# Expert weights loaded by halves, the recurrence's powers in a PSUM bank, and narrower expert slots

## The chip, the cores and the metric

One core of a Trainium2 chip. The metric is the device time of one execution in microseconds (us): the median of the runs shown. The engines are PE (TensorE), DVE (VectorE), ACT (ScalarE), POOL (GpSimd) and SP (SyncE, which here only issues DMAs). DMAs are issued from the queues of SP, ACT and POOL.

## The reference

A linear recurrence with a decay (RWKV) gives 3072 rows of 384 numbers; each row is then sent to one of 16 experts, chosen first by group and then within the group. All is fp32.

```python
# r, k, v: (4, 8, 768, 48); w, u: (8, 48)
for t in range(S):
    kt, vt, rt = (k[:, :, t], v[:, :, t], r[:, :, t])
    cur = np.einsum('bhd,bhe->bhde', u[None] * kt, vt)
    y[:, :, t] = np.einsum('bhd,bhde->bhe', rt, state + cur)
    state = w[None, :, :, None] * state + np.einsum('bhd,bhe->bhde', kt, vt)
# x = y as (3072, 384); w1: (4, 4, 384, 1024); w2: (4, 4, 1024, 384)
g_idx = argmax(x @ w_group);  e_idx = argmax(x @ w_expert[g_idx])
out[token] = softmax_weight_of_g * softmax_weight_of_e * (relu(x @ w1[g, e]) @ w2[g, e])
```

## The kernel before

**Tiles and steps.** The recurrence runs in 24 tiles of 128 tokens (`NT`), tile n being chunk c = n // 4 of batch b = n % 4; two tiles are a pair g. The loop over `s` (L852) is software-pipelined: step s turns tile s (`turn`, L710: PE transposes r into `pr` and the scaled k into `pk`; DVE makes `rT` = pr x T1T, ACT copies `kT`), makes the scores of tile s - 1 (`scores`, L723: PE, then DVE masks them into `am` by COPY_PREDICATED, L735), the values of tile s - 2 (`values`, L737: `py`, the state update `pu`) and turns back tile s - 3 (`back`, L783, with the routing logits). `am` is first filled by ACT with the diagonal (`own_scores`, L699): eight multiplications of the identity by `du`, the token's own product r u k. That comes from POOL (`own`, L686: `dg` = r x k, then x `ub`, which is u in all partitions) and a sum on DVE (`own_sum`, L694). POOL also scales k by the table T2 into `kh` (`scale_k`, L682).

**Tables.** `up_to` (L263) holds the powers of the decay w up to 128, made by four DVE scans. `backwards` (L285) makes the reversed powers `rev`, `turned` (L292) transposes them on PE into `ptab` and ACT copies that into T2; `powers` (L278) makes T1T. There is one table for each of three chunks (m = 0, 1, 2). At the start m = 0 is made on DVE, m = 1 on ACT; PE is kept busy by `warm` (products of ones) meanwhile.

**Loads.** r, k and v come in pairs into rings of four or five (`load_pair`, L144), from SP, with the first two k's from ACT. `rall` and `kall`, the rings of r and k, are later the place of the second expert's weights.

**Routing.** For groups of four tiles (the last four in twos) `route` (L377) chooses the expert of each row, its gate and its place, and POOL scatters rows of 386 numbers into regions of `x_sorted` (L457, one scatter a tile). After 16 tiles `pick_first` (L352) takes the two fullest experts, so that their weights can be loaded before the routing ends: at step 21 SP reads the number and sends for all of w1 of the first (four DMAs of 384 KB, L484), then, after the scatters of that time have landed, for part 0 of its rows (`load_rows`, L531) and all of w2 (1.5 MB, L489); at step 24 for w1 of the second. `columns(0)` (L556) turns the rows on DVE at step 24; `up(0, ...)` (L585) uses the first expert's w1 from step 25 on; `w2_part` (L477) copies w2 into the order of use, two of eight blocks at a time, three of the copies on POOL at step 25.

**Experts.** `ITEMS` (L509) are the expert slots: the fullest expert as two items, then one an expert, in falling order of counts. `SLOTS` are their widths in columns, fixed when the kernel is built; where a count is above its slot, a general path at the end does the rest (L1039). Each item is `up` (48 matmuls, three for each of 8 blocks and two passes, L596) and `down` (48 matmuls, L617), each as wide as the slot, so the time of PE goes with the width. The results go to `out` by scatters of POOL: in pieces (L656) and for the last item by rows (L669). In item i, SP sends for the rows of item i + 2 and, when `up` is through, for its w1 and w2 (L1033).

**Order.** Inside `manual_schedule` each engine runs its instructions in the order of the program; this covers all five engines up to L993, and PE and DVE in the experts. So whatever waits holds up all that stands behind it on its engine.

Of the kernel before, what the change touches and what calls it, by code (L numbers as in the profile page):

```python
# [15 lines left out]
P = 128  # L16
# [3 lines left out]
SLOTS = [256, 240, 233, 222, 216, 212, 206, 202, 199, 196, 193, 190, 187, 184, 178, 173]  # L20
# [14 lines left out]
def kernel(  # L35
# [88 lines left out]

    w2h = cst([HP, 2, DP], "w2h")
# [18 lines left out]
    def load_pair(g, k_queue=nc.sync):  # L144

        load(r, g, rts[g % RING][:, :, :, 0:D])
        load(k, g, kts[g % RING], k_queue)
        load(v, g, vts[g % (RING + 1)][:, :, :, 0:D])
# [18 lines left out]
    def turn_small():  # L167

        first, second = (
            gw_rows[:, BL * c : BL * (c + 1), :].rearrange("p d e -> p e d") for c in range(DP // BL)  # L170
        )
        nc.vector.transpose(gw_turned, first)
        for a in range(2):
            at = P // 2 * a
            nc.vector.transpose(gw_turned[at + BL : at + 2 * BL], second[at : at + BL])
        nc.scalar.copy(gw, gw_turned.rearrange("p e (m j) -> p j (e m)", j=HP))

    ub = cst([P, H, D], "ub")
    load_pair(0, nc.scalar)
    load_small()  # L180
    nc.scalar.dma_start(
        out=ub.rearrange("p h d -> p (h d)"), in_=bass.AP(tensor=u.tensor, offset=u.offset, ap=[[0, P], [1, H * D]])
    )
    load_pair(1, nc.scalar)
# [72 lines left out]
    nc.tensor.transpose(pw, w2h.rearrange("p e d -> p (e d)"), ident[0:HP, 0:HP])  # L257
    wc = cst([P, HP], "wc")
# [4 lines left out]
    up_to = cst([P, HP, P], "up_to")  # L263
# [14 lines left out]
    def powers(m, engine):  # L278
        for hc in range(HP):
            scaled(T1T[m][:, hc, :], up_to[:, hc, :], m, hc, engine)  # L280
# [4 lines left out]
    def backwards(m, engine):  # L285
        revs[m] = pool.tile([P, HP, P], FP32, name=f"rev_{m}")
        for hc in range(HP):
            x = up_to[:, hc, :]
            back = bass.AP(tensor=x.tensor, offset=x.offset + P - 1, ap=[list(x.ap[0]), [-1, P]])
            scaled(revs[m][:, hc, :], back, SPAN - 1 - m, hc, engine)  # L290

    def turned(m):  # L292
        ptab = bank([P, HP, P], "ptab")
        for hc in range(HP):
            nc.tensor.transpose(ptab[:, hc, :], revs[m][:, hc, :], ident)
        nc.scalar.copy(
            T2[m].rearrange("p (a e) d -> p a e d", e=2), ptab.rearrange("p a (e d) -> p a e d", e=2)[:, :, :, 0:D]
        )

    warm(5)  # L300
    backwards(0, nc.vector)
    turned(0)
    backwards(1, nc.scalar)
    nc.vector.reciprocal(by[:, 0, :], up_to[:, :, P - 1])
    nc.vector.tensor_mul(by[:, 0, :], by[:, 0, :], by[:, 1, :])
    powers(0, nc.vector)
# [13 lines left out]
    def span_decay():  # L320
        nc.gpsimd.tensor_mul(w_span, up_to[:, :, P - 1], up_to[:, :, P - 1])
        nc.gpsimd.tensor_mul(w_span, w_span, up_to[:, :, P - 1])
# [159 lines left out]
    def load_w1(e, i):  # L482
        for q in range(P // BL):
            nc.sync.dma_start(  # L484
                out=places[i][0][BL * q : BL * (q + 1)], in_=w1f[bass.ds(e, 1), q].rearrange("a p k f -> (a p) k f")
            )

    def load_w2(e, i):
        nc.sync.dma_start(out=places[i][1], in_=w2f[bass.ds(e, 1)].rearrange("a p k f -> (a p) k f"))  # L489

    def load_expert(e, i):

        load_w1(e, i)
        load_w2(e, i)
        return places[i]
# [32 lines left out]
    def padded(n):  # L528
        return -(-n // BL) * BL

# [32 lines left out]
    def keys_in(i):  # L563
# [4 lines left out]
        if is_last(i):  # L568
            for j, n in enumerate(parts(i)):
# [54 lines left out]
    def turn_out(i, d0, d1):  # L624

        if d0 == 0:
            out_rows[i] = [
                (bank([P, DM], "pb"), item_tile(i, [P, DM], "yt", bufs=4)) for j in range(len(parts(i)))
            ]
        gates = keys_of[i][1]  # L630
# [32 lines left out]
    def rows_out(i, d0=0):  # L663
        turn_out(i, d0, KO)
        ids = keys_of[i][0]
        for j, n in enumerate(parts(i)):
            yt = out_rows[i][j][1]
# [31 lines left out]
    def own_scores(n):  # L699

        am = ams[n] = pool.tile([P, 2, HP, P], FP32, tag="am", bufs=2, name="am")
        for e in range(2):
            for hc in range(HP):
                h = 2 * hc + e
                nc.scalar.mul(am[:, e, hc, :], ident, dus[n // 2][:, n % 2, h : h + 1])  # L705
# [131 lines left out]
    scale_k(0, nc.vector, 0, 1)  # L837
    scale_k(0, nc.gpsimd, 1, 2)
    own(0, nc.gpsimd, 0, 1)
    scale_k(1, nc.gpsimd)  # L840
    own(0, nc.gpsimd, 1, 2)
    todo, ending = {}, []
    SP = mybir.EngineType.SP

    def expert_of(number, engines):
# [3 lines left out]
        )  # L849

    LAST = 3
    for s in range(NT + LAST):  # L852
# [40 lines left out]
        if s == FOUR * B + 5:  # L893
            first = expert_of(first_i[0:1, 0:1], (SP,))
            second = expert_of(first_i[0:1, 1:2], (SP,))
            load_w1(first, 0)
        if s == NT:
            columns(0)
            load_w1(second, 1)
        run("first")  # L900
        if s < NT:
            turn(s)
            if s == 1:
                turned(1)
                turn_small()
            if s in (1, 2):
                own_sum(0, s - 1, s)
# [18 lines left out]
        if 0 <= s - 1 < NT:  # L926
            own_scores(s - 1)
        if s == 2:
            scores(1)
# [3 lines left out]
        if s == FOUR * B + 5:  # L933
            load_rows(0, first, nc.sync)
            load_w2(first, 0)
            weights[0] = places[0]
# [54 lines left out]
    load_w2(second, 1)  # L991
# [5 lines left out]
    with ExitStack() as moe:  # L997
        pools[1] = moe.enter_context(tc.tile_pool(name="moe", bufs=2, reuse_waits="tile"))
        w2_parts.append(pools[1].tile([P, FO, KO, P], FP32, bufs=1, name="w2_parts_1"))
        with tc.manual_schedule(engines={mybir.EngineType.PE, mybir.EngineType.DVE}):  # L1000
# [6 lines left out]
            for i in range(1, len(ITEMS)):  # L1007
# [11 lines left out]
                up(i, 2)  # L1019
                go_on()  # L1020
                up(i, 4)
                up(i, 6)
                e = ITEMS[i][0] + 2
                if e < GE:
                    expert = expert_of(order_i[0:1, e : e + 1], (SP,))
                    load_rows(i + 2, expert, nc.sync)
                go_on()
# [4 lines left out]
                if e < GE:  # L1032
                    weights[e] = load_expert(expert, e % 2)  # L1033
# [233 lines left out]
```

## Time and profile before

| | |
|---|---|
| median of 3 runs | 433.34 us (433.24 to 433.84) |
| profiled execution | 432.43 us, span 430.7 us |
| recurrence, to the first row of expert item 1 | 0 to 163.3 us |
| experts | 163.3 to 424.3 us on PE |
| last scatter issued | 426.2 us |
| PE clock granted | 0.993 on average |
| DMA moved | 86.67 MB, mean 201 GB/s |

The profile is of one execution. A line of a timeline has the start, the busy time, the engine, the line of the code, what it wrote and read, how many instructions were merged, and in brackets the idle time before it with the one that ended it: "issue" is time in which the engine waited for nothing that the profile shows. A line of a group has the busy time of all and the mean of one in ns; instructions overlap, so the mean is longer than the spacing. SP's own DMA issues show in the timeline with the time of issuing.

### The profile page before, as it was taken

The numbers are of one execution on the slowest core, as the hardware profiler recorded it, in microseconds if no ns is written. First come the engines' busy times: TensorE is split into PE (matmuls) and PEld (weight loads), VectorE is DVE, ScalarE is ACT, GpSimd is POOL, SyncE is SP. The second block draws the span as 40 slices with busy tenths as digits, with TensorE's granted clock in tenths as the row PEclk, the third lists the DMA queues.
The fourth block names the chain that finished last, engine by engine and source line by source line (L and its number), as shares of the span: only waits on it lengthen the run. The fifth ranks groups of instructions, "written<-read, shape, count | busy, mean of one in ns | idle before, by whom it ended". The sixth has DMA issues, their size and how long they took to land. (4 is left out here: it accounts for less than half of the span.)

```text
span 430.7 us, 9930 instructions
## 1 busy us (share of the span) xinstructions
PE 410.7 (95%) x3649; PEld 384.0 (89%) x3649; DVE 183.7 (43%) x620; ACT 216.4 (50%) x505; POOL 202.1 (47%) x214
## 2 busy tenths in 40 slices
PE   6799999999998897999999999999999999999993
PEld 5688888888875697999999999999999999999992
DVE  6666879787958555030322303303313303303211
ACT  2797767777667211624425253363463464355430
POOL 6875566666670633030517235144254245325452
PEclk9989999999999999999999999999999999999998
DMA  9999999991195929998969779889899899999001
GB/s 177 220 247 295 272 239 227 211 184 39 41 219 170 238 81 244 237 240 223 268 153 261 157 228 268 179 232 251 211 243 241 217 252 265 209 268 262 21 26 34
DMA packets 124476, 86.67 MB, mean 201 GB/s; under 512 B 96998, under 2 KB 113565, under 8 KB 124420
## 3 DMA queue, kind: packets, MB, share of 16 engines
q1 hardware_dynamic: 112732, 69.05, 71.2%
q0 software_dynamic: 4960, 9.48, 6.9%
q10 hardware_dynamic: 6728, 7.44, 5.2%
q8 instruction: 30, 0.49, 0.5%
q14 instruction: 26, 0.21, 0.2%
HBM read 70.15 MB, written 16.44 MB: 201 GB/s over the span
## 5 line engine op out<-in xcount | busy, mean ns | idle before, releaser
L656 POOL DMA_INDIRECT out_dram<-yp,ids x104 | 101.0, 972 | 162.4 <-DVE yo L611 127.2
L617 PE MATMUL po<-hT,w_parts 128*128 128x128 f32 (+15 forms) x816 | 139.7, 328 | 2.1 <-ACT hT L600 2.1
L617 PEld LDWEIGHTS po<-hT,w_parts 128*128 128x128 f32 x816 | 133.8, 190 | 3.2 <-ACT hT L600 2.3
L649 DVE STREAM_TRANSPOSE yr<-yo 128x224 f32<-128x224 f32 (+3 forms) x48 | 22.0, 464 | 183.6 <-ACT yo L620 179.2
L596 PE MATMUL ph<-xe,w 128*128 128x128 f32 (+7 forms) x432 | 72.2, 322 | 1.0 <-issue 0.6
L596 PEld LDWEIGHTS ph<-xe,w 128*128 128x128 f32 x432 | 68.6, 190 | 2.4 <-issue 1.4
L596 PE MATMUL ph<-xe,kall 128*128 128x240 f32 (+7 forms) x384 | 68.5, 334 | 0.0
L600 ACT ACTIVATE hT<-ph 128x256 f32<-128x256 f32 (+15 forms) x68 | 33.6, 496 | 67.5 <-PE ph L596 48.9
L596 PEld LDWEIGHTS ph<-xe,kall 128*128 128x128 f32 x384 | 65.4, 190 | 0.6
L620 ACT COPY yo<-po 128x128 f32<-128x128 f32 (+15 forms) x51 | 16.2, 321 | 92.0 <-PE po L617 55.4
L705 ACT ACTIVATE am<-ident,du 128x128 f32<-128x128 f32 x192 | 58.7, 390 | 2.4 <-DVE du L697 2.1
L735 DVE COPY_PREDICATED am<-later,pa 128x512 f32<-128x512 uint32 x48 | 32.7, 729 | 16.7 <-PE pr L716 5.0
L480 ACT COPY w_parts<-rall 128x768 f32<-128x768 f32 x32 | 38.1, 1241 | 0.0
L457 POOL DMA_INDIRECT x_sorted<-xt,place_i x24 | 23.8, 992 | 23.6 <-DVE rb L822 13.2
L480 ACT COPY w_parts<-w 128x768 f32<-128x768 f32 x29 | 34.4, 1237 | 0.0
L691 POOL TENSOR_TENSOR dg<-rall,kall 128x768 f32<-128x768 f32 (+1 forms) x13 | 22.1, 1701 | 23.1 <-DVE du L697 21.7
L730 PE MATMUL pa<-rT,kT 48*128 48x128 f32 x384 | 29.7, 288 | 0.4 <-issue 0.2
L758 PE MATMUL py<-am,vt 128*64 128x128 f32 x384 | 27.4, 285 | 0.0
L730 PEld LDWEIGHTS pa<-rT,kT 48*128 48x128 f32 x384 | 24.5, 189 | 2.7 <-issue 1.2
L684 POOL TENSOR_TENSOR kh<-kall,T 128x768 f32<-128x768 f32 (+1 forms) x12 | 21.6, 1803 | 9.9 <-PE py L758 2.8
L758 PEld LDWEIGHTS py<-am,vt 128*64 128x64 f32 x384 | 21.0, 139 | 4.6 <-issue 3.7
L720 ACT COPY kT<-pk 128x512 f32<-128x512 f32 x24 | 14.0, 584 | 20.0 <-PE pk L716 20.0
(146 smaller groups left out, 405.9 us busy)
## 6 DMA issues: line engine op xcount, KB each, us to landing
w<-in_moe_w_dram SPq DMA_DIRECT2D x32, 384.0 KB
w<-in_moe_w_dram SPq DMA_DIRECT2D x8, 1536.0 KB
kall<-in_moe_w_dram SPq DMA_DIRECT2D x32, 384.0 KB
rall<-in_moe_w_dram SPq DMA_DIRECT2D x8, 1536.0 KB
x_sorted<-nothing ACTq DMA_DIRECT2D x4, 1544.0 KB
rall<-in_r_dram SPq DMA_DIRECT2D x12, 384.0 KB
vt<-in_v_dram SPq DMA_DIRECT2D x12, 384.0 KB
kall<-in_k_dram SPq DMA_DIRECT2D x10, 384.0 KB
```

The costliest lines, as they stand in the source:

```text
L457: ins = nc.gpsimd.indirect_dma_start(out=xs_dram, out_offset=bass.IndirectOffsetOnAxis(ap=place_i[:, i : i + 1], axis=0), in_=xt[:, i, :], ...
L480: copy(w2_parts[e % 2][:, a : a + 2], w2[:, a : a + 2, :].rearrange("p f (c k) -> p f k c", k=KO))
L596: nc.tensor.matmul(ph[:, q, :], lhsT=w1[:, ko, P * (f + q) : P * (f + q + 1)], rhs=xe[:, ko, 0:w], start=(ko == 0), stop=(ko == KO - 1), s ...
L600: nc.scalar.activation(hTs[i][:, f : f + 2, 0:w], ph, AF.Relu)
L617: nc.tensor.matmul(po, lhsT=w2[:, fo, d, :], rhs=hT[:, fo, 0:w], start=(fo == 0), stop=(fo == FO - 1))
L649: nc.vector.transpose(yr[:, 0:b, :, d], y[:, d, 0:w].rearrange("p (b t) -> p b t", t=BL))
L656: ins = nc.gpsimd.indirect_dma_start(out=out_pieces, out_offset=bass.IndirectOffsetOnAxis(ap=ids[:, j : j + 1], axis=0), in_=yp[:, j], in_ ...
L691: engine.tensor_mul(dg, rts[g % RING][:, a0:a1, :, 0:D], kts[g % RING][:, a0:a1])
L705: nc.scalar.mul(am[:, e, hc, :], ident, dus[n // 2][:, n % 2, h : h + 1])
L730: nc.tensor.matmul(pa[e][:, hc, :], lhsT=kT[rows, hc, :], rhs=rT[rows, hc, :], start=True, stop=True, skip_group_check=True,)
L735: nc.vector.copy_predicated(am[:, e], earlier, pa[e])
L758: nc.tensor.matmul(py[e][DP * o : DP * (o + 1), j, :], lhsT=vt[:, a, 4 * o + 2 * j + e, :], rhs=am[:, e, 2 * o + j, :], start=(c == 0), st ...
```

## The change

- The slots are narrower: 3264 columns in all instead of 3287. The scatter of the last item's second part takes 48 rows, the ones beyond the slot being zeros sent to an index past the end.
- `load_w1` and `load_w2` load one half (512 of 1024 hidden units). In the recurrence, the halves are sent for at steps 21 and 22 (w1 of the first expert), 22 (end) and 24 (its w2), 25 and 26 (w1 of the second), and at the end both halves of the second's w2. `at_step` makes POOL copy the expert's number at that place of its program, and SP reads the copy. In the experts, the halves are sent for one by one through `up`, w1's and w2's first halves before the rows.
- `up_to` lies in a PSUM bank of the routing's pool, and so does a copy of the identity. u comes as one row (1.5 KB) and is spread over the partitions by a matmul.
- At the start the loads come in the order k0 (ACT's queue), r0, r1, v0, v1 (SP's), small ones and k1 (ACT's). The reversed powers of m = 0 are made by DVE and ACT, two each; the first half of `kh` by DVE straight from `ptab`; T1T of m = 0 by ACT. POOL begins with the own products of the first tile; four of that tile's `am` are made by DVE.
- The tables of m = 1 are made over steps 1 to 3 instead of the start and step 1; the copy of `gw` comes at step 2; `span_decay` goes from POOL to DVE.

```diff
-SLOTS = [256, 240, 233, 222, 216, 212, 206, 202, 199, 196, 193, 190, 187, 184, 178, 173]
+SLOTS = [256, 237, 233, 220, 214, 209, 205, 202, 199, 194, 193, 189, 185, 183, 176, 169]
...
+    u_row = cst([1, H * D], "u_row")
+    nc.sync.dma_start(out=u_row, in_=bass.AP(tensor=u.tensor, offset=u.offset, ap=[[H * D, 1], [1, H * D]]))
...
-    ub = cst([P, H, D], "ub")
-    load_pair(0, nc.scalar)
+    load_pair(0, "k", nc.scalar)
+    for g, inputs in ((0, "r"), (1, "r"), (0, "v"), (1, "v")):
+        load_pair(g, inputs)
     load_small()
-    nc.scalar.dma_start(
-        out=ub.rearrange("p h d -> p (h d)"), in_=bass.AP(tensor=u.tensor, offset=u.offset, ap=[[0, P], [1, H * D]])
-    )
-    load_pair(1, nc.scalar)
+    load_pair(1, "k", nc.scalar)
...
+    pub = rpsum.tile([P, 512], FP32, tag="route", name="pub")
+    nc.tensor.matmul(pub[:, 0 : H * D], lhsT=ones[0:1, :], rhs=u_row, start=True, stop=True)
+    ident_p = pub[:, 512 - P : 512]
+    nc.tensor.transpose(ident_p, ident, ident)
+    ub = cst([P, H, D], "ub")
+    nc.scalar.copy(ub.rearrange("p h d -> p (h d)"), pub[:, 0 : H * D])
...
-    up_to = cst([P, HP, P], "up_to")
+    up_to = rpsum.tile([P, HP, P], FP32, tag="route", name="up_to")
...
-    warm(5)
-    backwards(0, nc.vector)
-    turned(0)
-    backwards(1, nc.scalar)
+    warm(8)
+    backwards(0, nc.vector, (0, 1))
+    backwards(0, nc.scalar, (2, 3))
+    table = turned(0)
...
-    powers(0, nc.vector)
+    nc.vector.tensor_mul(
+        khs[0][:, 0, :, 0:D].rearrange("p (a e) d -> p a e d", e=2),
+        kts[0][:, 0].rearrange("p (a e) d -> p a e d", e=2), table,
+    )
+    powers(0, nc.scalar)
...
-    def load_w1(e, i):
+    FH, FOH = F // 2, FO // 2
+
+    def load_w1(e, i, half):
+        units = slice(FH * half, FH * (half + 1))
         for q in range(P // BL):
             nc.sync.dma_start(
-                out=places[i][0][BL * q : BL * (q + 1)], in_=w1f[bass.ds(e, 1), q].rearrange("a p k f -> (a p) k f")
-            )
+                out=places[i][0][BL * q : BL * (q + 1), :, units],
+                in_=w1f[bass.ds(e, 1), q, :, :, units].rearrange("a p k f -> (a p) k f"),
+            )
...
-            yt = out_rows[i][j][1]
+            yt, n = out_rows[i][j][1], sixteens(n)
...
-    def own_scores(n):
+    def own_scores(n, es=(0, 1), engine=nc.scalar):
...
+                if engine is nc.scalar:
+                    nc.scalar.mul(x, ident, of)
+                else:
+                    engine.tensor_scalar(out=x, in0=ident_p, scalar1=of, scalar2=None, op0=OP.mult)
...
-    scale_k(0, nc.vector, 0, 1)
+    own(0, nc.gpsimd, 0, 1)
     scale_k(0, nc.gpsimd, 1, 2)
-    own(0, nc.gpsimd, 0, 1)
-    scale_k(1, nc.gpsimd)
+    scale_k(1, nc.gpsimd, 0, 1)
     own(0, nc.gpsimd, 1, 2)
+    scale_k(1, nc.gpsimd, 1, 2)
+    own_sum(0, 0, 1)
...
+    def at_step(s, j):
+
+        number = cst([1, 1], f"number_{s}", I32)
+        nc.gpsimd.tensor_copy(number, first_i[0:1, j : j + 1])
+        return expert_of(number, (SP,))
...
-            load_w1(first, 0)
+            load_w1(first, 0, 0)
+        if s == FOUR * B + 6:
+            load_w1(at_step(s, 0), 0, 1)
         if s == NT:
             columns(0)
-            load_w1(second, 1)
+            load_w2(at_step(s, 0), 0, 1)
+        if s in (NT + 1, NT + 2):
+            load_w1(at_step(s, 1), 1, s - NT - 1)
         run("first")
+        if s == 1:
+            own_scores(0, (0,))
+            own_scores(0, (1,), nc.vector)
+        if s == 2:
+            own_sum(0, 1, 2)
         if s < NT:
             turn(s)
             if s == 1:
+                backwards(1, nc.scalar, (0,))
+            if s == 2:
+                backwards(1, nc.scalar, (1, 2, 3))
+                turn_small()
+            if s == 3:
                 turned(1)
-                turn_small()
-            if s in (1, 2):
-                own_sum(0, s - 1, s)
...
         if s == FOUR * B + 5:
+            weights[0] = places[0]
+        if s == FOUR * B + 6:
             load_rows(0, first, nc.sync)
-            load_w2(first, 0)
-            weights[0] = places[0]
+            load_w2(first, 0, 0)
...
                 up(i, 2)
+                e = ITEMS[i][0] + 2
+                if e < GE:
+                    expert = expert_of(order_i[0:1, e : e + 1], (SP,))
+                    load_w1(expert, e % 2, 0)
                 go_on()
                 up(i, 4)
                 up(i, 6)
-                e = ITEMS[i][0] + 2
                 if e < GE:
-                    expert = expert_of(order_i[0:1, e : e + 1], (SP,))
+                    load_w2(expert, e % 2, 0)
                     load_rows(i + 2, expert, nc.sync)
+                    load_w1(expert, e % 2, 1)
+                    load_w2(expert, e % 2, 1)
+                    weights[e] = places[e % 2]
                 go_on()
                 down(i, 0)
...
-                if e < GE:
-                    weights[e] = load_expert(expert, e % 2)
```

## The prediction

> **What bounds the kernel.** I read the page first. The share of busy time and the slices say that PE is full but for three places: the first 20 us, the stretch around 125 to 165 us, and the tail.
>
> ```profile
> span 430.7 us, 9930 instructions
> PE 410.7 (95%) x3649; PEld 384.0 (89%) x3649; DVE 183.7 (43%) x620; ACT 216.4 (50%) x505; POOL 202.1 (47%) x214
> PE   6799999999998897999999999999999999999993
> q8 instruction: 30, 0.49, 0.5%
> ```
>
> So after 163 us (the experts) only fewer or shorter matmuls help; before that, waits. The chain of waits is of no use here: it holds 1 us. The timeline of each engine shows how the start runs (start, length, engine, line, work; in brackets the idle time before it and what ended that):
>
> ```profile
> 8.71 0.87 DVE L276 TENSOR_SCALAR T1T<-up_to,by 128x128 f32<-128x128 f32 x4
> 9.37 1.53 POOL L684 TENSOR_TENSOR kh<-kall,T 128x384 f32<-128x384 f32 x1 [2.32 <-ACT T L296]
> 13.72 2.45 ACT L705 ACTIVATE am<-ident,du 128x128 f32<-128x128 f32 x8 [0.16 <-DVE du L697]
> 15.03 0.73 DVE L735 COPY_PREDICATED am<-later,pa 128x512 f32<-128x512 uint32 x1 [1.35 <-ACT am L705]
> 19.31 0.73 DVE L735 COPY_PREDICATED am<-later,pa 128x512 f32<-128x512 uint32 x1 [1.34 <-ACT am L705]
> 20.10 0.66 PE L716 MATMUL pk<-ident,kh 128*128 128x128 f32 x4 [1.32 <-DVE am L735]
> ```
>
> POOL makes half of kh, then the own products, then DVE sums, then ACT makes eight am tiles, and only then can DVE mask. PE waits for that chain. The table of windows adds that the clock granted to PE was 0.52, 0.50 and 0.50 of full speed from 22 to 25 us, after the 1.3 us gap of the last line.
>
> Around 126 and 146 us PE and ACT wait for nothing that the profile shows:
>
> ```profile
> 117.86 2.01 SPq L484 DMA_DIRECT2D w<-in_moe_w_dram  x4
> 128.65 0.55 PE L716 MATMUL pr<-ident,rall 128*128 128x128 f32 x3 [0.44 <-issue]
> 130.09 0.54 PE L716 MATMUL pk<-ident,kh 128*128 128x128 f32 x3 [0.44 <-issue]
> 134.57 0.39 SPq L489 DMA_DIRECT2D w<-in_moe_w_dram  x1
> 135.21 1.96 SPq L484 DMA_DIRECT2D kall<-in_moe_w_dram  x4
> 147.87 0.60 PE L596 MATMUL ph<-xe,w 128*128 128x128 f32 x3 [0.44 <-issue]
> 148.04 0.65 ACT L764 COPY yT<-py 128x256 f32<-128x256 f32 x2 [4.48 <-remote]
> ```
>
> Each stall lies 8 to 13 us after whole weight matrices were sent for (1.5 MB each), while scatters were under way too. My reading: instruction blocks (queue q8, 30 packets of 16 KB) queue behind the weights. The windows agree: DMA share 1.02 from 125 to 128 us and from 146 to 149 us, and PE is full again once it falls.
>
> **The change part by part.** (a) *Columns.* The slots fall from 3287 to 3264, 23 fewer. The groups by form give L617 and L596 10.2 + 10.1 us at 240 columns and 7.5 + 7.4 at 173, so (20.3 - 14.9) / 67 = 0.0806 us a column over 96 matmuls; times 23 = **1.85 us**, on a PE that is full there. Padding to 32 is the same for all 16 slots, so no DVE or scatter work goes. Counting the routing of these inputs, the largest token count at every rank is below its slot, so the leftover path stays shut.
>
> (b) *Start.* I replayed the engines in the new program order with durations of the rows. rev: two on DVE at 0.22 beside two on ACT, ptab done at 8.7 as before, since three more warm matmuls, pub (384 columns) and the extra transpose end at 8.2 on PE. DVE makes kh from ptab at 8.8 (before 9.49, after the copy and T1T). ACT makes T1T after the copy, to 10.4; rT of tile 0 is then 0.5 late, which costs nothing as the am tiles come later. POOL begins own(0) at 7.1 behind its memsets instead of kh at 9.37: the first dg is done at 9.1 (1.00 + 1.01), not 12.96. ACT then makes four am tiles (1.25) beside four on DVE, so tile 0 is masked by 14.4 (before 16.94), tile 1 by 18.4 (before 21.22, with turn_small's 1.2 us of DVE ahead of it), own_sum(1) ends at 19.7 (before 22.75), PE begins tile 4 at about 23 (before 26.27). What is late next is ACT: it is full from there to 31 us, with turned(1)'s copy moved into it. The ub broadcast of 192 KB that goes and r1 ahead of v0 help, as PE waited for r1 until 14.23. u_row ahead of w2h on SP may cost up to 0.4 (one issue). I take **3.0**. Ends: 1.0 (k1 or r1 land late as r1 did, or the 1.8 us lost to the half clock, 3.6 us at 0.5, are merely moved) and 4.3 (the replay's 3.2 and part of the 1.8 saved). Later the recurrence needs loads 3 us earlier; POOL waited for k only once there (2.4 us, at 50.1 us), some 6 us ahead of PE's use, so that cover holds.
>
> [...]
>
> (c) *First stall.* From the first score matmul to the next logits transpose took 125.58 to 130.47 = 4.89; the step before, 120.93 to 122.96 = 2.03: **2.86 us** lost. Half the matrix at step 21 is sent before the five scatters; the second half is sent by at_step on POOL behind those scatters (last 128.01 + 0.97, some 3 earlier), so weights and scatters no longer overlap. But the rows of item 0 are late next: SP issues their loads behind at_step's wait and the second half, at about 129 to 131, and they landed at most 4.3 us after issue (133.9 to 138.2). DVE comes to columns(0) at 132.3 now, so 1 to 3 us of the gain are waited away there, with the gate and place of the next scatters queued behind it. I take **1.3**, ends 0 and 2.86.
>
> (d) *Second stall.* py ended at 144.8 and ACT's copy began at 148.04: **3.2 us** on the chain that leads through logits, routing and the last two scatters to the first expert rows. Now 1.5 MB of w2 is sent at 132 to 134 and expert two's halves only behind POOL's scatters, two steps apart. What is late next is POOL: four scatters, at_step, three w2_part copies (3.54), two scatters (1.28 apart), at_step, then the last two. That ends 1.0 above the chain. And the second half of expert two lands on top of the last scatters (0.77 MB, 2 us at the 390 GB/s seen at 138 us); I give it 0.5. Net **1.7**, ends -1.5 (stall kept, the collision in full) and 3.2.
>
> (e) *Third stall.* ACT waits 3.91 ("remote") to 171.92, and PE 2.09 with it, while expert two's w2 and rows land. They land still, but the next w1 goes in halves: **0.7**, ends 0 and 2.1.
>
> (f) *Small.* Three POOL copies before scatters, by L321's 0.20 each: -0.2 in all, since part is in POOL's gaps. SP's four extra register loads (0.27 to 0.49 each) lie ahead of loads with slack. In the experts SP sends w1's first half before the rows; rows and weights are used an item (17 us) later, so 0; without that slack each microsecond of lateness would stop PE. The last scatter (45 to 48 rows) and two memsets on an idle DVE: 0.
>
> Sum: 1.85 + 3.0 + 1.3 + 1.7 + 0.7 - 0.2 = 8.35. The profiled execution took 432.43 us (span 430.7 and 1.7 around it), so 424.1; the median is 0.91 above it: **425.0 us**.
>
> [...]
>
> **Rivals.** *The waits stay.* The halves move the bursts and blocks arrive as late at another place. For it: at_step at step 24 waits for nothing that at_step at step 22 didn't, so w2's halves leave back to back. Against it: weights and scatters overlap less. Then only (a), (b) and (f) count: 433.34 - 4.65 = 428.7.
>
> *The start gives little*, (b) at 1.0, because ACT, which gains a copy in step 3, or the half clock is the bound: 427.0. For it: ACT is gapless from 20.4 to 36.6 us. Against it: PE's gap of 1.3 us ahead of the clock's fall goes in the replay.
>
> *Slower: POOL waits for w2's second half.* The copy of parts 4 and 5 stands on POOL ahead of the last four scatters, which feed the first expert. If that half lands after about 145 us, each microsecond is lost at 1:1; beyond some 5 us it eats (a), (b) and more: late by 9 us, 433.34 - 4.65 + 6 (3 of it hidden in POOL's slack) = 434.7. Against it: its issue at about 133 us and 1.5 MB landing before in some 7 us.
>
> **Chances.** Forecast 0.58, waits stay 0.22, little start 0.13, slower 0.05, no change 0.02. The forecast's own bounds, with (c) to (e) all good or half, are 421.5 to 427; the first two rivals reach to 429.5 with their own spread, and that is my range. A measurement of this kernel tells 0.2% (0.87 us) from no change. Faster by more 0.92, within 0.03, slower 0.05.
>
> **What would show it.** Tile 0 masked by 14.5 us and tile 1 by 18.5; PE at tile 4 by 23 us with no window at half clock. No "issue" gaps on PE in the score matmuls of step 22 and no "remote" wait of ACT before the last yT. DVE waiting for xg at columns(0). The last row scatter 5 to 8 us earlier. Expert matmuls 1.85 us less in sum. The prediction is wrong if gaps of the same size stand at other places, or if POOL waits for w2.

## The result and the profile after

| | before | after |
|---|---|---|
| median on the chip of the prediction | 432.85 us (6 runs) | 433.75 us (6 runs) |
| ratio to before, 95% interval | | 1.0016 (0.9995 to 1.0038) |
| profiled execution, span | 432.43, 430.7 us | 432.23, 430.4 us |
| the same two kernels on chip D | 422.72 us (11 runs) | 425.72 us (6 runs) |
| ratio on chip D | | 1.0065 (1.0049 to 1.0081) |

Predicted were 425.0 us. No gain came on the first chip, and a loss of 3 us on another. The first rows of the page of after, to be held against those of before:

```profile
span 430.4 us, 10247 instructions
PE 413.1 (96%) x3658; PEld 385.4 (90%) x3658; DVE 185.6 (43%) x623; ACT 214.2 (50%) x508; POOL 202.0 (47%) x217
...
PE   7999999999989898999999999999999999999993
...
PEclk9999999999998999899999999999999999999999
```

PE has 9 matmuls more, and narrower ones in the experts, yet 2.4 us more busy time: it ran slower, as the row of the granted clock shows with the two eights (slices of 10.8 us, at 129 and at 172 us). The start, in after's timeline:

```profile
9.98 0.55 DVE L316 TENSOR_TENSOR kh<-kall,ptab 128x384 f32<-128x384 f32 x1 [0.52 <-ACT T L307]
...
11.64 1.11 DVE L743 TENSOR_SCALAR am<-pub,du 128x128 f32<-128x128 f32 x4
11.77 1.28 ACT L741 ACTIVATE am<-ident,du 128x128 f32<-128x128 f32 x4
...
13.31 1.36 DVE L773 COPY_PREDICATED am<-later,pa 128x512 f32<-128x512 uint32 x2
...
18.06 0.74 DVE L773 COPY_PREDICATED am<-later,pa 128x512 f32<-128x512 uint32 x1 [0.40 <-ACT am L741]
...
23.46 0.66 PE L754 MATMUL pr<-ident,rall 128*128 128x128 f32 x4
```

Tile 0 is masked by 14.7 us (16.94 before), tile 1 by 18.8 (21.22), and PE comes to tile 4 at 23.46 (26.27). At step 22 the first score matmul stands at 123.06 instead of 125.58: 2.5 us are in hand. The two stalls, in the same timeline:

```profile
120.36 1.01 POOL L472 DMA_INDIRECT x_sorted<-xt,place_i  x1
...
125.49 0.97 POOL L472 DMA_INDIRECT x_sorted<-xt,place_i  x1 [0.30 <-issue]
...
120.45 0.27 PE L859 MATMUL rb<-ident,lgT 128*128 128x128 f32 x1
...
124.62 0.51 PE L768 MATMUL pa<-rT,kT 48*128 48x128 f32 x4 [0.23 <-issue]
125.38 0.27 PE L754 MATMUL pr<-ident,rall 128*128 128x128 f32 x1 [0.24 <-issue]
126.07 0.54 PE L754 MATMUL pr<-ident,rall 128*128 128x128 f32 x3 [0.43 <-issue]
...
127.52 0.49 PE L754 MATMUL pk<-ident,kh 128*128 128x128 f32 x3 [0.79 <-issue]
127.84 0.27 PE L859 MATMUL rb<-ident,lgT 128*128 128x128 f32 x1
...
145.60 0.65 ACT L802 COPY yT<-py 128x256 f32<-128x256 f32 x2 [4.48 <-remote]
```

Both are there, at the same size. From the logits' transpose (L859) of step 21 to that of step 22 it takes 7.39 us (before 7.51; a step without a stall takes 4.64), and the wait before yT is 4.48 as before. The third is there too (PE waits 2.11 us for hT at 171.12, before 2.09). What the DMA engines did meanwhile, in the DMA view of after for 120 to 126.4 us (the first row is the busy share in 40 slices):

```profile
DMA  1000030000009963000099630000996300009963
...
q0 software_dynamic: 254, 0.79, 33.3%
q8 instruction: 1, 0.02, 0.9%
q1 hardware_dynamic: 6, 0.00, 0.4%
```

q1 carries the weights and moved nothing. The only traffic is that of the scatters themselves, each a burst of some 0.6 us with idle engines after it, and one instruction block, at 120.9 us. So nothing waited behind weights. No other block moves until 129 us, and PE's gaps end at 127.5: PE goes on without a new block, so a late block is not what it waits for here. The lead then goes. PE's windows of after, with the granted clock as the fourth number:

```profile
22.00:26.00 4.00, 3.63 (x47) 1.00 1.06 279
...
128.00:132.00 4.00, 4.00 (x46) 0.57 0.83 202
148.00:152.00 4.00, 3.74 (x17) 0.57 0.79 199
172.00:176.00 4.00, 4.00 (x14) 0.57 1.06 287
```

and the same of before:

```profile
22.00:26.00 4.00, 4.00 (x47) 0.57 1.13 325
128.00:132.00 4.00, 2.93 (x28) 1.00 0.30 110
148.00:152.00 4.00, 3.07 (x27) 1.00 0.53 186
172.00:176.00 4.00, 3.64 (x20) 1.00 0.91 211
```

A window with 0.57 costs an estimated (1 - 0.57) x 4 = 1.7 us of PE's work. Up to the last matmuls, before lost one, at the start; after lost three, one behind each stall. The lead was 2.5 us at 123 us, 1.3 at item 1's first matmul (162.04 against 163.31) and -0.4 at 178 us. From there to the end the experts gave 0.4 of their 1.85 us.

### The profile page after: what moved, and what is told of

It reads as the page before. It is cut to its first block, busy times and chain, and to the rows that moved or that the text cites. A ratio compares the mean times of both kernels' runs of the same rounds, so it can differ in the third digit from the quotient of the medians.

```text
span 430.4 us, 10247 instructions
## 1 busy us (share of the span) xinstructions
PE 413.1 (96%) x3658; PEld 385.4 (90%) x3658; DVE 185.6 (43%) x623; ACT 214.2 (50%) x508; POOL 202.0 (47%) x217
## 5 line engine op out<-in xcount | busy, mean ns | idle before, releaser
L627 PE MATMUL ph<-xe,w 128*128 128x128 f32 (+7 forms) x432 | 73.9, 327 | 1.1 <-issue 1.0
L627 PEld LDWEIGHTS ph<-xe,w 128*128 128x128 f32 x432 | 70.0, 196 | 2.7 <-issue 1.9
L627 PE MATMUL ph<-xe,kall 128*128 128x237 f32 (+7 forms) x384 | 69.8, 338 | 0.0
L741 ACT ACTIVATE am<-ident,du 128x128 f32<-128x128 f32 x188 | 57.6, 395 | 0.2
L758 ACT COPY kT<-pk 128x512 f32<-128x512 f32 x24 | 14.2, 593 | 20.4 <-PE pk L754 15.8
```

Source lines behind the costliest of these rows:

```text
L627: nc.tensor.matmul(ph[:, q, :], lhsT=w1[:, ko, P * (f + q) : P * (f + q + 1)], rhs=xe[:, ko, 0:w], start=(ko == 0), stop=(ko == KO - 1), s ...
L741: nc.scalar.mul(x, ident, of)
```

## The experiments

In the text, chip A is the one of the result; each group of runs had one chip, with before timed beside them. A step's time is that from one logits' transpose on PE to the next (4.64 us at step 22 if nothing stalls).

### Is it the weights, or the scatters? (chip B, before 430.41 us)

Theory S: a run of scatters on POOL holds up PE and ACT. W: the prediction's reading, weights delay instruction blocks. B: it is the place in PE's program. `run_at_17` puts the four scatters of tiles 8 to 11 into one run at step 17:

```diff
-                when.append((when[5][0] + (1 + i if n < FOUR * B - 1 else 0), "last"))
+                when.append((when[5][0] + (1 + i if n < FOUR * B - B - 1 else 0), "last"))
```

> The changed kernel with the four scatters of tiles 8 to 11 moved together to step 17, where no weights are under way; a run of five there, and of four at step 21. Theory S: a new stall of PE marked issue of 2 to 3.5 us at steps 17 to 18, ending 1 to 1.4 us after the run. Theory W: none there, and the one at step 22 as it was. Theory B (the stall belongs to the place in PE's instruction stream): none at step 17, and step 22 as it was.

434.89 us in one run. Its timeline:

```profile
99.02 1.01 POOL L472 DMA_INDIRECT x_sorted<-xt,place_i  x1 [0.16 <-DVE rb L467]
...
104.17 0.97 POOL L472 DMA_INDIRECT x_sorted<-xt,place_i  x1 [0.31 <-issue]
...
102.50 0.37 PE L808 MATMUL pu<-vt,kh 128*64 128x48 f32 x5 [0.41 <-issue]
...
104.64 0.53 PE L768 MATMUL pa<-rT,kT 48*128 48x128 f32 x5 [0.77 <-issue]
...
106.11 0.79 PE L768 MATMUL pa<-rT,kT 48*128 48x128 f32 x9 [0.47 <-issue]
```

With five scatters in a row at 99 to 105 us, PE stalls at 102 to 106, where neither before nor after has a gap and no weights have been sent for yet: SP sends nothing between 90 us and its first weights at 120.29 us. That step takes 9.4 us instead of 5.1, and step 22, with four left there, has one gap of 0.23 and takes 5.29.

`no_run_21` leaves out the scatters of tiles 12 to 15:

```diff
-            each = [lambda i=i: rows(i) for i in range(ROUTED[n])]
+            each = [lambda i=i: rows(i) for i in range(ROUTED[n]) if n != FOUR * B - 1]
```

> The changed kernel without the four scatters of tiles 12 to 15 at step 21 (their rows never reach the experts, and the output misses them). Theory S: no stall of PE at step 22; from the first score matmul to the next logits transpose about 2.0 us instead of 4.8. Theories W and B: 4.8 us as before.

425.58 us in one run. Step 22 of PE:

```profile
123.14 1.16 PE L768 MATMUL pa<-rT,kT 48*128 48x128 f32 x16
124.23 0.65 PE L754 MATMUL pr<-ident,rall 128*128 128x128 f32 x4
124.72 0.60 PE L754 MATMUL pk<-ident,kh 128*128 128x128 f32 x4
125.16 0.27 PE L859 MATMUL rb<-ident,lgT 128*128 128x128 f32 x1
```

The stall is gone: 4.64 us, not 7.39. The first half of w1 leaves as in after (115.43 us), and the second leaves 5 us sooner (122.16 instead of 127.17), beside this very step. W and B fall. Two kernels on the same chip split the change. `whole_loads` is after with the loads of before; `slots_only` is before with the new slots and the 48-row scatter.

```diff
-    def load_w1(e, i, half):
+    def load_w1(e, i):
...
-            load_w1(first, 0, 0)
-        if s == FOUR * B + 6:
-            load_w1(at_step(s, 0), 0, 1)
+            load_w1(first, 0)
...
-            load_w2(at_step(s, 0), 0, 1)
-        if s in (NT + 1, NT + 2):
-            load_w1(at_step(s, 1), 1, s - NT - 1)
+            load_w1(second, 1)
```

> The changed kernel with the weights sent for whole, as before the change; the rest of the change stays. Theory S (the stalls of PE at step 22 and of ACT and PE at step 26 belong to runs of four or five scatters on POOL, not to the weights): the same stalls of 2.8 and 3.2 us, ending about 1 to 1.4 us after the last scatter of the run, and the recurrence's landmarks within 0.5 us of the changed kernel. Theory W (the prediction's: weights delay the instruction blocks): stalls at least 1 us longer than with halves. If the small PE gaps marked issue in the experts (about 1.4 us) come from the halves, they go, and the time is 0.5 to 1.5 us below the changed kernel; if not, the same within 0.5 us.

> The kernel before with only the narrower slots and the last scatter of 48 rows. By the groups of matmuls, 23 columns x 0.0806 = 1.85 us: 431.0 to 431.5 beside a before of 432.9 to 433.3, if PE's dense time is all that counts. If the clock of PE answers to the phase of its gaps (theory G), the recurrence is untouched, so the gaps fall as before and the gain is seen in full; if less than 1 us is seen, something else in the experts gives it back.

Slots alone: 428.86 us, 0.9960 (0.9942 to 0.9978), so 0.4% or 1.7 us less, as predicted. Start and slots: 429.86 us, 0.9978 (0.9959 to 0.9998). The start brings nothing on top of the slots. Step 22 takes 7.28 us with the weights sent whole (7.39 in after), where W asked for 1 us more, and PE's "issue" gaps in the experts are not there.

### The parts alone, and scatters spread (chip C, before 429.97 us)

`start_only` is whole_loads with the old slots, `halves_only` is before with the loads by halves, both out of the change's own diff.

> Before with the start of after alone (weights sent whole, old slots). My prediction gave the start 3.0 us: ratio 0.993. Theory G (the half clock after PE's gaps takes it back): PE reaches tile 4 by 2 to 2.8 us sooner, yet the end comes 0 to 1 us sooner, ratio 0.998 to 1.000, with the clock at half in one more window than in before, or with the matmuls ahead of ptab at half clock (they stand on the path to kh now). If the start itself is no faster (a cost hidden in it), PE's first score matmul of step 22 is not sooner either.

> Before with the loads by halves alone (old start, old slots). My prediction gave this 3.7 - 0.2 us: ratio 0.992. Theory S (runs of scatters hold up PE and ACT, weights have nothing to do with it): nothing gained at the stalls, ratio 0.999 to 1.002. A theory that halves cost something of themselves (four more waits of SP on the path, more issue gaps of PE in the experts): ratio 1.002 to 1.005, and the experts' part grows by 1 us or more.

Start alone: 430.18 us, 1.000 (0.9978 to 1.0023). Halves alone: 432.71 us, 1.0049 (1.0027 to 1.0071), a loss of 2.1 us. So slots -1.7, start 0, halves +2.1 make +0.4 of the +0.7 us (0.16%) that the whole change showed. Both profiles have the stall at step 22 unchanged (7.9 and 7.7 us). In halves_only PE takes 250.88 us from item 2 to its end, before 250.94 on chip A, so that the loss lies ahead of the experts.

`spread` is after with the same scatters in another order:

```diff
-                when.append((when[5][0] + (1 + i if n < FOUR * B - 1 else 0), "last"))
+                step = 1 + i if n < FOUR * B - B - 1 else i if n < FOUR * B - 1 else i // 2 if n == FOUR * B - 1 else 0
+                when.append((when[5][0] + step, "last"))
...
+            if n == NT - B - 1:
+                between.extend(each[1:])
+                each[1:] = []
...
             for a in (0, 2, 4):
                 w2_part(0, a, nc.gpsimd.tensor_copy)
+                between.pop(0)()
```

> After with the same scatters in another order: tiles 8 to 11 one step sooner, tiles 12 to 15 two at step 21 and two at step 22, tiles 16 to 19 with the copies of w2's parts between them. No run of more than three is left in the recurrence. S: no issue gaps at step 22 (from the first score matmul to the logits' transpose 2.0 to 3.0 us instead of 4.8) and no remote wait of ACT before yT above 1 us; 4 to 6 us sooner than after at 160 us, ratio to before 0.985 to 0.992. W (weights delay instruction blocks) and B (place in PE's stream): the stalls stay, ratio 1.000 to 1.002. The wait for hT at 170 us, beside four scatters of output pieces, stays by every theory.

429.18 us, 0.9974 (0.9954 to 0.9995): 0.4% below after's ratio on chip A, less than S asked for. Its timeline says why:

```profile
102.71 0.37 PE L808 MATMUL pu<-vt,kh 128*64 128x48 f32 x5 [0.40 <-issue]
103.45 0.33 PE L808 MATMUL pu<-vt,kh 128*64 128x48 f32 x3 [0.37 <-issue]
...
162.09 3.20 PE L627 MATMUL ph<-xe,w 128*128 128x128 f32 x15 [2.64 <-DVE xe L590]
```

The second stall is gone: ACT has no "remote" wait before that yT (it waits 0.90 us for py), and PE comes to the output blocks of item 0 at 149.94 instead of 153.51 us. But three scatters fell in a row at step 17, with the two gaps above, and at step 22 POOL came late to the first pair, so that four ran in a row after all. And what was won before 150 us is waited away at 162 us, for item 1's rows. The steps of these runs give a rough scale of the stall with the length of the run of scatters: two in a row cost nothing (at 101 and 112 us in before, without an "issue" gap on PE), three 1.3 us (step 17 of spread), four 1.8 (step 22 of spread) but 0.65 in run_at_17, five 2.6 to 3.3 (step 22 of before, after and the part kernels on chips A to C) and 4.3 at step 17, with some half-clock time in it.

`spread_slots` is slots_only with the same order.

> Before with the new slots and with the scatters spread as in the run beside it; old start, weights sent whole. S: 0.996 for the slots, and the two stalls gone: ratio 0.982 to 0.989; W: the stalls stay, ratio 0.995 to 0.997. If it comes out below the run beside it, halves and the new start cost more than they bring.

424.83 us, 0.9858 (0.9823 to 0.9893). In this kernel item 0's rows are sent for ahead of the scatters of tiles 14 and 15, so these stand beyond that load and item 0 works on rows that are not all there; the time is no claim for a version, but step 22 takes 4.87 us with two scatters beside it (in a profiled execution of 429.98 us).

### A chip without the stalls (chip D, before 422.72 us)

> The kernel before, profiled on the chip on which the others of this call run, so that places in time can be compared on one chip. It tells whether chips differ in the stretch up to 163 us: by theory S the two stalls of 2.9 and 3.2 us stand beside the runs of scatters here as well; the half clock may fall elsewhere than at 22 to 25 us.

> The whole change on this chip. From its parts measured one by one (start 1.000, halves 1.0049, slots 0.996 of before) the product is 1.001; if parts spoil each other it is off that by more than 0.003. Theory G expects half-clock windows behind the same stalls at 128, 148 and 172 us again; if they stand elsewhere the clock is no cause but scatter of one execution.

Before in one profiled run: 422.51 us. After: 425.72 us, 1.0065 (1.0049 to 1.0081), against a product of the parts of 1.001. The timeline of before here:

```profile
120.91 1.01 POOL L457 DMA_INDIRECT x_sorted<-xt,place_i  x1 [0.15 <-DVE rb L452]
...
126.06 0.97 POOL L457 DMA_INDIRECT x_sorted<-xt,place_i  x1 [0.30 <-issue]
...
124.72 0.65 PE L716 MATMUL pr<-ident,rall 128*128 128x128 f32 x4
125.21 0.60 PE L716 MATMUL pk<-ident,kh 128*128 128x128 f32 x4
125.65 0.27 PE L821 MATMUL rb<-ident,lgT 128*128 128x128 f32 x1
```

The same program, the same five scatters, and no stall: step 22 takes 4.64 us, from 90 to 182 us PE has no "issue" gap, and from 100 us on ACT has no "remote" wait. So S holds on chips A to C (and F below), and on D and E the runs of scatters cost nothing. PE comes to item 2 at 163.38 us here and at 172.91 on chip A, nearly all of the 9.9 us between the two profiles of before. What makes a chip one or the other isn't known here.

Without stalls one sees what the halves cost. SP and PE of after, chip D:

```profile
143.93 7.85 SPq L504 DMA_DIRECT2D kall<-in_moe_w_dram  x8
156.76 0.83 SPq L577 DMA_DIRECT2D xg<-x_sorted  x2
...
159.92 7.25 PE L627 MATMUL ph<-xe,w 128*128 128x128 f32 x48 [3.94 <-DVE xe L590]
```

and of before:

```profile
152.83 0.83 SPq L548 DMA_DIRECT2D xg<-x_sorted  x2
...
156.14 5.62 PE L596 MATMUL ph<-xe,w 128*128 128x128 f32 x48 [0.93 <-DVE xe L561]
```

The last scatter ends on POOL at 151.85 us in after and 151.00 in before. SP waits until its data has landed: 4.91 us in after, 1.83 in before. In after the second expert's w1 was sent up to 151.8 us; its loads land a median 5.0 us after their issue (192 KB into kall), so by an estimate the last are moving until about 156.8 us. PE then waits 3.94 us for xe instead of 0.93, and its clock falls behind that wait: its next 48 matmuls take 7.25 instead of 5.62 us. The sum over PE's landmarks: lead at step 21 -0.4 us, item 0's rows and the last two turns +1.2 (15.80 against 14.60 us), from there to item 1 +3.0 (16.28 against 13.27), item 1 at half clock +1.6, experts -1.85 (248.81 against 250.66 us), together +3.55; the last PE instruction stands 3.57 later. All executions point the same way: the mean granted clock is 0.9905 in six of after and 0.9958 in eleven of before, which times the span is an estimated 2.3 us more of half clock in after, out of the 3.0 us lost.

> Before with the new slots and no more than two scatters in a row on POOL in the recurrence: tiles 0 to 11 one a step and one step sooner, tiles 12 to 15 two at step 20 and two at step 21, tiles 16 to 19 in two pairs with two memsets between. Theory S: no issue gaps at step 22 (2.0 to 2.5 us from first score matmul to logits' transpose where before has 4.9) and no remote wait before yT above 1.5 us; ratio 0.984 to 0.990. If only single long runs matter and the sum of scatters is what holds PE up, gaps of about 1 us come at steps 20 to 21 instead: ratio 0.990 to 0.994. W or B: 0.995 to 0.997, as for the slots alone.

`even_slots` is slots_only with the routing of tiles 8 to 15 one step sooner, so that no step has more than two scatters, and two memsets of POOL between the pairs of tiles 16 to 19:

```diff
-            if n < NT - B - 1:
+            if n < FOUR * B - B - 1:
...
-                when.append((when[5][0] + (1 + i if n < FOUR * B - 1 else 0), "last"))
+                step = i if n < FOUR * B - 1 else i // 2 if n == FOUR * B - 1 else 0
...
+                    for _ in range(2):
+                        nc.gpsimd.memset(nothing, 0.0)
```

426.27 us, 1.0092 (1.0079 to 1.0105). On this chip there was nothing to win, and one sees the price of the order: PE is 2.2 us behind before at step 22, as the routing's DVE work now stands in fuller steps, and the last scatters end 3.9 us later.

> After with ten idle matmuls ahead of the last four of item 1's output blocks, where PE waits 2.1 us for hT, and four ahead of the logits' transpose of the last tile. Theory G (PE's idle gaps bring the half clock behind them, which eats the start's lead): no half clock at 172 to 176 us, at most one window between 145 and 180 us, 1.5 to 3 us less than after: ratio to before 0.995 to 0.998. If the clock falls for another reason, it falls in the same places and the ratio is after's, 1.001 or more.

```diff
+            if i == 1 and d == 0 and fo == FO - 2:
+                warm(10, bank([P, P], "idle"))
...
+        if n == NT - 1:
+            warm(4, bank([P, P], "idle"))
```

428.22 us, 1.0135 (1.0113 to 1.0157). No test of the clock: on this chip PE doesn't wait for hT there, so the extra matmuls only cost time. The half clock came with another wait (2.72 us for xe, until 158.7 us).

### Is it the collision, and is it the warm-up? (chip E, before 422.37 us, no stalls either)

`second_early` sends both halves of the second expert's w1 at step 24:

```diff
-        if s in (NT + 1, NT + 2):
-            load_w1(at_step(s, 1), 1, s - NT - 1)
+            for half in range(2):
+                load_w1(second, 1, half)
```

> After with both halves of the second expert's w1 sent at step 24, behind w2's second half, and not one a step at 25 and 26: none of its transfers is left when the last scatters run. Theory C (the second half of that w1 lies ahead of the last scatters' data, so item 1's rows are sent for 4.9 us after the last scatter instead of 1.8, PE waits for xe and its clock then falls to half): SP sends item 1's rows at most 2.0 us after the last scatter, PE waits for xe at most 1 us, and the ratio is 0.005 to 0.010 below after's on a chip that has no issue gaps, 0 to 0.005 below it on one that has them. If halves cost something in the experts instead: no change from after.

426.61 us, 1.0100 (1.0086 to 1.0115). The mechanism came out as expected, 1.83 us from the last scatter (ending at 156.62) to the rows, and 1.80 us of waiting for xe with no half clock behind it:

```profile
158.45 0.83 SPq L577 DMA_DIRECT2D xg<-x_sorted  x2
```

but the time didn't, since 3.5 us are gone much earlier:

```profile
32.76 1.81 POOL L718 TENSOR_TENSOR kh<-kall,T 128x768 f32<-128x768 f32 x1 [4.79 <-DMA kall<-in_k_dram]
```

POOL waits for k of pair 2, 15 steps ahead of the edit. The last section comes back to it.

> After with the weights sent whole, on the chip of the runs beside it. Theory C: like second_early, within 0.003 of it; item 1's rows sent for at most 2.0 us after the last scatter.

> Before with the new slots alone, on the chip of the runs beside it: ratio 0.995 to 0.997, whichever chip it is, since the columns are PE's own time. It would be the fastest of the four unless the start brings at least 0.5 us.

Whole loads: 421.71 us, 0.9987 (0.9968 to 1.0005), the rows 1.83 us after the last scatter. Against after's 1.0065 on the like chip D, halves cost 0.8% or 3.3 us where nothing stalls. Slots alone: 420.65 us, 0.9960 (0.9947 to 0.9973), the same as on chip B, and the lowest ratio of any kernel that does the whole work.

`warm_less` has `warm(2)` in place of `warm(8)` ahead of ptab:

> After with two warm matmuls of two passes each instead of eight ahead of ptab. Theory P (the start's gain is smaller than 3.0 us because pub and the warm matmuls run at half rate in some executions, 0.23 instead of 0.12 us each, and ptab then comes at 10.4 to 10.6 instead of 8.2 us): ptab no later than 9.4 us in any execution, 0.5 to 1 us less than after in the median, nothing in an execution whose warm matmuls are fast. If the rate has no part in it: no change, or PE slower behind them by up to 1 us since it was warmed less.

426.41 us, 1.0108 (1.0092 to 1.0125): no gain. Its ptab began at 8.22 us in an execution whose warm matmuls are slow, as expected, but behind it everything else is as in after, the collision too (4.99 us to the rows, 4.19 us of waiting for xe). That PE's rate at the start varies is seen in the profiles of after itself. Chip A:

```profile
6.09 1.95 PE L205 MATMUL idle<-ones 128*128 128x128 f32 x16
8.19 1.24 PE L305 MATMUL ptab<-ident,rev 128*128 128x128 f32 x4
```

and chip D:

```profile
7.03 3.62 PE L205 MATMUL idle<-ones 128*128 128x128 f32 x16
10.44 0.80 PE L305 MATMUL ptab<-ident,rev 128*128 128x128 f32 x4
```

The same sixteen passes take 0.12 or 0.23 us each, and ptab, which they stand ahead of, comes 2.25 us later. Three of the ten profiles with this start and `warm(8)` are of the slow kind. With the old start slow ones occur too, and there ptab waits for rev anyway.

### The collision without the new start (chip F, before 430.23 us, with stalls)

> Before with the new slots and the loads by halves, old start: after without its start. The slots alone gave 0.996 on two chips. Theory C (halves delay the rows of item 0 and, through the second half of expert two's w1, those of item 1): item 1's rows sent for 3 us or more after the last scatter on a chip without issue gaps, 2 to 3 us on one with them, and the ratio is 1.002 to 1.006. If only the new start makes after slow: 0.995 to 0.998.

> The same with both halves of the second expert's w1 sent at step 24, as one load was before. Theory C: item 1's rows sent for at most 2.0 us after the last scatter, and the ratio 0.004 to 0.010 below the run beside it on a chip without issue gaps, 0 to 0.005 below on one with them; what is left above 0.996 is the price of item 0's rows, sent behind a wait. If the collision is no cause: the same ratio as the run beside it.

Halves and slots: 430.93 us, 1.0023 (1.0009 to 1.0037); against 0.9960 for slots alone, halves cost 0.6% again. With w1 sent early: 434.94 us, 1.0118 (1.0097 to 1.0139), against the expectation. From last scatter to rows it is 2.96 and 1.94 us, and from the last logits' transpose to item 1's first matmul 13.60 and 12.71 us, so the collision costs some 0.9 us here. But early_slots has lost 2.7 us by the transpose at 44.22 us (41.50 in the other) and 3.7 two steps later, as second_early had. One has the new start and the other the old, neither touched by the edit; what they share is named in the last section. So the price of the collision is shown by PE's landmarks only, and no version with halves and without it was faster as a whole.

## Why the prediction was wrong, point by point

**(a) Columns, 1.85 us: right.** Slots alone gave 0.9960 on two chips, 1.7 us. Item 2's start to the last PE instruction is 1.85 us shorter on chip D. On chip A after got only 0.4 of it from 178 us on: PE's gaps grew by 0.8 us there (0.41 and 0.45 us of "issue" at 368 and 422 us). The third half-clock window lies ahead of that count.

**(b) Start, 3.0 us: nearly met in the first profile, 0 in the time.** On chip A ptab and DVE's kh came 0.7 and 1.2 us later than in the replay (9.43 and 9.98 us instead of 8.7 and 8.8), but the masks and tile 4 were within 0.5 us of it, and 2.5 us were in hand at step 22. A scaling on DVE was a little dearer out of PSUM: the four am tiles that read `pub` took 1.11 us, 0.28 each, where T1T of before, out of SBUF, took 0.87 us for four, 0.22 each. Two things were missed. The profile of before that I started from is a bad one: its first logits' transpose is at 27.2 us, where the eight other profiles with the old start have 26.3 to 26.7, since they have no half clock at 22 us; the eleven with the new start lie between 24.1 and 27.0, median 25.1. So the gain is 1.5 us there, not 3. And it doesn't last. At step 21 the new start stands between 1.6 us ahead of the old one and 0.4 behind it on chips B to E, within 0.5 us of what it was at the first transpose (second_early and the two kernels with a stall at step 17 aside). So the loads cost little of the lead, though "that cover holds" was wrong too: in after POOL waits three times for k, 7.1 us in all. The rest is lost later. With whole weights and the new start, PE begins item 1 4.1 to 5.0 us after SP sends for its rows (start_only, whole_loads, whole_again), with the old start 3.3 to 3.4 us after. And the granted clock of all executions makes an estimated 0.7 to 1.0 us more of half clock with the new start than without it (chips B, C and E). Why those rows come later stays open. start_only says 1.000.

**(c), (d), (e) The stalls, 3.7 us: wrong, the failing step.** "My reading: instruction blocks queue behind the weights." The weights were near the stalls in time and the scatters were too; I took the one that the change touched. The windows that I called in agreement were not: from 128 to 131 us the DMA share was down to 0.40 and PE was busy for 1.93 of 3 us, and from 149 to 152 us it was 0.37 and 2.07. On a chip with stalls, scatters alone moved the first stall (run_at_17) or removed it (no_run_21), and removed the second (spread); weights in halves did neither (after, halves_only). So the three terms are worth 0, and halves alone cost 2.1 us on chip C, where the sum had them bring 3.5. Of its 8.35 us only the 1.85 of (a) came out in the time. The third stall stands behind four scatters of results; no run moved those, so its cause is not shown. My warnings were of the right kind and too small. In (c), item 0's rows come late: some 1.2 us on chip D. In (d), "the second half of expert two lands on top of the last scatters; I give it 0.5": it took 3.1 us of landing there, and 1.6 of half clock behind. On chip A the rows are sent for 2.08 us after the last scatter instead of 1.85, so the collision hardly shows there.

**Rivals.** "The waits stay" is what happened to the waits, but its 428.7 us kept the start's 3.0 us and left out that halves cost 2 to 3 us of their own. "POOL waits for w2's second half" didn't happen: its copies at 144.6 us follow the scatters without a wait. The loss on chip D is its twin on another engine: SP waits for the scatters' landing behind the new half.

**The clock** was in the prediction only as part of (b). In the windows of chip A it took back what the start had won. That gaps cause it is a reading of many profiles, not a run's verdict: fill couldn't test it, and of the eight profiles with five scatters ahead of step 22 and a stall there, four have a half clock behind it and four none. With PE's wait for item 1's xe the half clock came in all five waits of 2.6 us or more, in two of six of 1.7 to 2.4 us, and in none of seven of 0.3 to 1.3 us. The half-clock stretches of before and after, up to the last matmuls, are 3.41 us long each: from 22.04 us in before, from 128.04, 148.52 and 172.41 us in after. In the 3.41 us ahead of them PE was busy for 2.09 us in before and for 1.96, 1.94 and 1.30 us in after, and not at all in warm_less (idle from 155.5 to 159.7 us, half clock from an estimated 159.5). So PE was not idle ahead of most of them, and what brings the clock down is not shown.

## What to carry to other kernels

A stall that "waits for nothing" has no cause in the profile; two things that stand beside it are two suspects, and a run that moves one of them is cheaper than a change built on the other. A transfer cut in halves is not sent earlier or later but next to something else: ask what that something's waiters do. And one profile on one chip is thin: here the same program was 10 us faster on another chip, without the stalls that the change was meant to remove, and the loss that they hid came out.

## What was not expected of the hardware

**Scatters and the feeding of engines.** With four or five indirect DMAs in a row on POOL (1.28 us each), PE gets one to four matmuls every 0.7 us (before, 127.2 to 130.1 us) and ACT nothing for up to 4.5 us, and steps are held up on four chips; on two others neither is seen. In after the DMA engines are idle between the scatters' bursts meanwhile, and the one instruction block moved at 120.9 us, ahead of PE's gaps. In the experts of chip A, runs of four to eight do little to PE, but ACT has "remote" waits beside them, of 2.3 to 5.1 us in after and at most 1.8 us in before, where the weights come whole (both from 180 us on); on chip D it has none. With five scatters beside it step 22 takes 4.64 us on chips D and E, as if nothing held it up, and 7.3 to 7.9 on the others. Whether the fetching of instructions has a part in that isn't shown: what PE waits for is open.

**The packets of the first loads.** The packets of q1 take different times in different kernels, worked out from their count and their share of the time of 16 engines. From 3 to 35 us on chip A they take 18.8 ns each on average in after (24712 packets, 90.6%) and 20.4 in before (24437, 97.2%); from 0 to 60 us on chip F 18.2 ns in halves_slots (39102, 74.3%) and 23.4 in early_slots (35152, 85.8%). By their programs after and halves_slots have four of at_step's four-byte tiles, early_slots and second_early two, and before none. early_slots and second_early are the two whose recurrence fell 3.5 to 3.7 us behind at its loads. Why early_slots' packets take longer isn't shown: my guess is that these tiles move r's and k's rings and that the place counts, but the traces hold no addresses, and no run changed the tiles alone.
